# An opening written out engine by engine: attention of three pieces, the first weight halves and TensorE's fillers in one fixed order

## The chip, the cores and the metric

The kernel runs on one core of one Trainium2 chip. The metric is the device time of one execution in microseconds. Before the change it is 868.75 us, the median of three runs (868.51 to 876.98).

## What is computed

Sparse attention over 4 batches, 8 heads, 576 positions and 64 dimensions feeds two feed-forward layers over all 2304 tokens (512 to 2048 to 512), one behind the other. Heads 0 to 3 look at a local window of 32, heads 4 to 7 at positions of the same remainder modulo 32:

```python
scores = np.where(masks, scale * q @ k.T, -1e9); attn = softmax(scores)   # sum + 1e-9
x = (attn @ v).transpose(0, 2, 1, 3).reshape(2304, 512)
h = np.maximum(x @ w_in, 0.0);  x = h * h @ w_out                          # first layer
h = x @ w_in2                                                              # second layer
g = (a0 + a1*h + a2*h**2 + a3*h**3) / (1 + |b0|*|h| + |b1|*h**2 + 1e-6)
out = g @ w_out2
```

The weights arrive as 64-bit floats.

## The kernel before

**Work.** Tokens are cut into six blocks (WIDTHS: 512, 256, then four of 384). For each block j and each of 16 slices f of the hidden width, a unit (j, f) makes 12 products of the first matrix (`h_unit`, line 418: four slices kk of x, each with wh·xh, wh·xl, wl·xh, since every operand is split into a high part that the fast format holds and a low rest), then the square of the ReLU on ScalarE (ACT) and VectorE (DVE), and two units later 12 products of the second matrix (`o_unit1`, line 463). The second layer follows in the same manner (`unit2`). In block 0 a product has 512 columns.

**Attention** goes in 14 pieces, strided ("s") or local ("l"). A piece is scored (`at_scores`: a mask product, line 292, then products of q and k, line 297, into two banks r = 0, 1), normalised bank by bank (`at_softmax`: maximum, subtraction on DVE, exponential on ACT, sum, inverse on DVE, scaling on GpSimd, lines 327 to 341), transposed on TensorE and copied by ACT (`at_transpose`, lines 349, 351), multiplied with v (`at_values`, line 358), and split into xh (a cast on ACT, line 380) and xl (a subtraction on DVE, line 382) by `at_out`. P0, P1 (both strided) and P2 (local) are done ahead of unit (0, 0). P0 and P1 fill the slices kk = 2, 3 of x in block 0, P2 fills kk = 0, 1. The other pieces stand between later units, at the units that the table PLAN names for scores, transposes and values.

**Weights.** `feed_w` takes the halves of the first layer's weights in the order `wq` (first matrix of f, second matrix of f some units behind it): the raw 64-bit words come by DMA, ACT scales the upper word (line 185), DVE joins the bits in three operations (186 to 188), GpSimd makes the high part (197) and the low part (198). Three halves are fed ahead of unit (0, 0), then two per unit.

**What sets the order.** The program is recorded line by line and a scheduling layer then puts the instructions of each engine in order; each engine runs its own queue strictly in that order. Instructions given to `keep_in_program_order` keep the order in which they are written. Before, these are TensorE's instructions of P0 to P2 and the fillers (`fill`, line 486: products of a tile of ones that no one reads, 128x512 in bf16, as many as FILL says at each place). The queue of DMA loads is SP's; a load past `under_way` bytes waits for an earlier one.

Of the kernel before, what the change touches and what calls it, by code (L numbers as in the profile page):

```python
# [9 lines left out]
F32 = mybir.dt.float32  # L10
# [8 lines left out]
P = 128  # L19
# [35 lines left out]
FILL = {'s0': 8, 's1': 1, 't00': 6, 't01': 2, 's2': 2, 't10': 2, 'v1': 4, 't20': 4, 't21': 2, 'h0': 3}  # L55
# [63 lines left out]
def moe_kernel(ctx, tc, qs, vs, ql, vl, w1, w2, a, b, masks, eye, out):  # L119
# [74 lines left out]

    def split_w(wh, wl, wf):
# [78 lines left out]
    def at_scores(p):  # L274

        for r in range(2):
            p.ps[r] = acc_bank(f"ps_s{p.name}_{r}", r == 0 and p.n > HEAD and PLAN[p.n][0][0] == 2)
        late = p.n >= MASK_PE
        fill(f"s{p.n}", p.ps[0])
        masks_ = []  # L280
        for r in range(2):
# [29 lines left out]
        for m in range(p.cb):  # L311
            for hp in range(2):
                for c in range(4):
                    j = 4 * m + c
                    k0 = WIDTHS[p.at] + STARTS[p.at] - _key_start(p.at) + _local_window(p.at, j)
                    for r in range(2):
                        x = p.qk[hp][r * D : (r + 1) * D]
                        score(r, c * STRIDE, 2 * m + hp, x[:, j * STRIDE : (j + 1) * STRIDE], x[:, k0 : k0 + EW])
# [25 lines left out]
    def at_transpose(p, r):  # L344
# [6 lines left out]
        nc.scalar.copy(p.t[r], ps[:, : p.cb * P])  # L351
# [24 lines left out]
    def split_x(parts):  # L376


        for dst, src in parts:
            nc.scalar.copy(dst[0], src)  # L380
        for dst, src in parts:
            nc.vector.tensor_tensor(dst[1], src, dst[0].bitcast(F32), ALU.subtract)

    def at_out(p):
        if not p.strided:
            w = WIDTHS[p.at]
            x_half(0, p.at, 0)
            split_x([(x_rows(0, p.at, hp, w), p.o[hp][:, :w]) for hp in range(2)])
            return
# [16 lines left out]
        split_x([(views, src) for _, views, src in sorted(parts, key=lambda t: t[0])])  # L406
# [75 lines left out]
    def fill(what, ps):  # L482


        for _ in range(FILL.get(what, 0)):
# [5 lines left out]
    load_qk(pieces[1])  # L491
    load_v(pieces[0])
    load(ident, eye)
    load_qk(pieces[2])
# [44 lines left out]
    P0, P1, P2 = pieces[:HEAD]  # L539
    at_scores(P0)  # L540
    at_softmax(P0, 0)
    at_softmax(P0, 1)
    at_scores(P1)
    at_softmax(P1, 0)
    at_transpose(P0, 0)
    at_softmax(P1, 1)
    at_transpose(P0, 1)
    at_scores(P2)
    at_softmax(P2, 0)
    at_values(P0)  # L550
    at_softmax(P2, 1)
    load_qk(pieces[3])
    at_out(P0)
    feed_w(1)
    at_transpose(P1, 0)
    at_transpose(P1, 1)
    at_values(P1)
    at_out(P1)
    load_v(pieces[3])
    feed_w(1)  # L560
    at_transpose(P2, 0)
    at_transpose(P2, 1)
    at_values(P2)
    at_out(P2)
    phase, under_way[0] = 1, 0
    load_raw(fed[0])
    feed_w(1)
# [17 lines left out]
    keep = tc.keep_in_program_order  # L585
# [77 lines left out]
    def unit2(j, f):  # L663
# [105 lines left out]
```

## Time and profile before

| | us |
|---|---|
| median of three runs | 868.75 (868.51 to 876.98) |
| the profiled execution | 869.74 |
| its span, first to last instruction | 868.0 |
| TensorE busy | 857.1 (99%) |
| VectorE, ScalarE, GpSimd busy | 609.8, 482.7, 540.1 |

The profile is of one execution. Times in its rows count from the start of the span, 1.7 us of the execution lie outside it. PE is TensorE's products, PEld its weight loads, DVE is VectorE, ACT ScalarE, POOL GpSimd, SP the engine that issues the DMAs. "Idle before" is the time for which the engine stood still ahead of a row, and what ended it. Rows of several instructions in a row are merged: "0.94 ... x48" is 0.94 us from the first one's start to the last one's end, and products overlap.

### The profile page before, as it was taken

The numbers are of one execution on the slowest core, as the hardware profiler recorded it, in microseconds if no ns is written. First come the engines' busy times: TensorE is split into PE (matmuls) and PEld (weight loads), VectorE is DVE, ScalarE is ACT, GpSimd is POOL, SyncE is SP. The second block draws the span as 40 slices with busy tenths as digits, with TensorE's granted clock in tenths as the row PEclk, the third lists the DMA queues.
The fourth block names the chain that finished last, engine by engine and source line by source line (L and its number), as shares of the span: only waits on it lengthen the run. The fifth ranks groups of instructions, "written<-read, shape, count | busy, mean of one in ns | idle before, by whom it ended". The sixth has DMA issues, their size and how long they took to land.

```text
span 868.0 us, 16453 instructions
## 1 busy us (share of the span) xinstructions
PE 857.1 (99%) x6333; PEld 789.0 (91%) x6338; DVE 609.8 (70%) x791; ACT 482.7 (56%) x1009; POOL 540.1 (62%) x563
## 2 busy tenths in 40 slices
PE   7999999999999999999999999999999999999998
PEld 4788889999999999999999999999999999999996
DVE  6899947635656555452135898888888888888884
ACT  4555633333333334332246877767777767876763
POOL 2677736535554555563324877777777877777773
PEclk9999999999999999999999999999999999999999
DMA  9982345535554445645765200100100100100101
GB/s 330 356 269 90 111 153 186 195 98 172 158 191 154 143 150 189 195 147 184 267 228 208 77 9 10 56 10 10 56 10 10 55 10 10 37 1 0 37 1 37
DMA packets 38959, 100.09 MB, mean 115 GB/s; under 512 B 4576, under 2 KB 10464, under 8 KB 38880
## 3 DMA queue, kind: packets, MB, share of 16 engines
q1 hardware_dynamic: 38880, 99.04, 34.1%
q8 instruction: 50, 0.82, 0.4%
q14 instruction: 29, 0.24, 0.1%
HBM read 72.80 MB, written 26.21 MB: 114 GB/s over the span
## 4 chain that ended last, share of the span: by engine, by line
PE 98%; DVE 1%; POOL 0%; ACT 0%; issue 0%; ACTq 0%; POOLq 0%
PE h L418 46%; PE acc L649 23%; PE acc L463 23%; PE ps_vl L358 1%; PE ps_sl L297 1%; PE ps_vs L358 1%; PE ps_ss L297 1%; PE ps_ts L349 1%; PE ps_tl L349 0%; PE ps_ss L486 0%; DVE sm L327 0%; DVE sm L338 0%; PE ps_tl L486 0%; PE ps_ss L292 0%; DVE eal L336 0%
## 5 line engine op out<-in xcount | busy, mean ns | idle before, releaser
L418 PE MATMUL h<-xh,wh 128*128 128x384 f32 (+2 forms) x768 | 260.4, 339 | 0.7 <-DVE rq L627 0.7
L418 PE MATMUL h<-xh,wl 128*128 128x384 f32 (+2 forms) x768 | 258.1, 336 | 0.0
L418 PE MATMUL h<-xl,wh 128*128 128x384 f32 (+2 forms) x768 | 257.7, 336 | 0.0
L618 DVE RECIPROCAL h<-w 128x384 f32<-128x384 f32 x96 | 245.1, 2553 | 0.7 <-POOL w L615 0.7
L614 POOL TENSOR_TENSOR p<-p,hs 128x384 f32<-128x384 f32 x96 | 98.8, 1029 | 102.4 <-ACT p L612 102.4
L418 PEld LDWEIGHTS h<-xh,wh 128*128 128x128 f32 x768 | 144.8, 189 | 8.2 <-DVE rq L627 1.0
L418 PEld LDWEIGHTS h<-xl,wh 128*128 128x128 f32 x768 | 144.6, 188 | 6.3
L418 PEld LDWEIGHTS h<-xh,wl 128*128 128x128 f32 x768 | 144.4, 188 | 2.6
L463 PE MATMUL acc<-gh,wh 128*128 128x384 f32 (+2 forms) x384 | 128.8, 337 | 0.0
L463 PE MATMUL acc<-gh,wl 128*128 128x384 f32 (+2 forms) x384 | 128.6, 335 | 0.0
L463 PE MATMUL acc<-gl,wh 128*128 128x384 f32 (+2 forms) x384 | 128.6, 335 | 0.0
L441 POOL TENSOR_TENSOR gl<-r,gh 128x384 fp32r<-128x384 f32 (+1 forms) x75 | 74.5, 996 | 73.0 <-ACT gh L440 68.9
L649 PE MATMUL acc<-wh,gl 128*128 128x512 f32 x288 | 113.9, 395 | 0.0
L649 PE MATMUL acc<-wl,gh 128*128 128x512 f32 x288 | 113.7, 395 | 0.0
L649 PE MATMUL acc<-wh,gh 128*128 128x512 f32 x288 | 111.9, 389 | 0.0
L437 DVE TENSOR_TENSOR r<-r 128x384 f32<-128x384 f32 (+1 forms) x75 | 49.5, 661 | 86.6 <-ACT r L433 86.5
L609 ACT ACTIVATE sq<-h 128x384 f32<-128x384 f32 x96 | 47.8, 498 | 105.8 <-PE h L418 101.4
L616 DVE SCALAR_TENSOR_TENSOR p<-p,co,h 128x384 f32<-128x384 f32 x96 | 58.4, 608 | 63.4 <-POOL p L614 63.4
L635 POOL TENSOR_TENSOR gl<-rq,gh 128x384 fp32r<-128x384 f32 x96 | 99.2, 1033 | 2.0 <-ACT gh L634 2.0
L615 POOL TENSOR_TENSOR w<-w,sq 128x384 f32<-128x384 f32 x96 | 98.7, 1029 | 0.0
L433 ACT ACTIVATE r<-h 128x384 f32<-128x384 f32 (+2 forms) x91 | 44.4, 488 | 88.3 <-PE h L418 88.2
L440 ACT CAST gh<-r 128x384 fp32r<-128x384 f32 (+2 forms) x91 | 46.7, 513 | 84.2 <-DVE r L437 83.4
(109 smaller groups left out, 1369.2 us busy)
## 6 DMA issues: line engine op xcount, KB each, us to landing
wraw<-in_w SPq DMA_DIRECT2D x64, 512.0 KB, 4.4
w_scratch<-sph SPq DMA_DIRECT2D x32, 256.0 KB, 3.9
w_scratch<-spl SPq DMA_DIRECT2D x32, 256.0 KB, 3.2
wh<-w_scratch SPq DMA_DIRECT2D x16, 512.0 KB, 3.7
wl<-w_scratch SPq DMA_DIRECT2D x16, 512.0 KB, 4.6
qks<-in_qs SPq DMA_DIRECT2D x8, 585.0 KB, 5.8
xraw<-x_scratch SPq DMA_DIRECT2D x24, 192.0 KB, 2.4
out_dram<-osb SPq DMA_DIRECT2D x18, 256.0 KB, 2.2
```

Of the source, the lines that this page charges most:

```text
L418: nc.tensor.matmul(ps[:, :n], w[:, c], x, start=(kk == 0 and i == 0), stop=(kk == KT - 1 and i == 2))
L437: nc.vector.tensor_tensor(h, h, h, ALU.mult)
L440: last_act = nc.scalar.copy(gh, h).ins
L441: low = lambda: (nc.vector if psum_h or j == 0 else nc.gpsimd).tensor_tensor(gl, h, gh.bitcast(F32), ALU.subtract)
L463: nc.tensor.matmul(acc[j][e][:, : WIDTHS[j]], w[:, c], g, start=(f == 0 and i == 0), stop=(f == NF - 1 and i == 2))
L609: keep(nc.scalar.activation(sq, h, AF.Square))
L614: keep(nc.gpsimd.tensor_tensor(p1, p1, hs, ALU.mult))
L615: keep(nc.gpsimd.tensor_tensor(w, w, sq, ALU.add))
L616: keep(nc.vector.scalar_tensor_tensor(p1, p1, a1, h, ALU.add, ALU.mult))
L618: keep(nc.vector.reciprocal(h, w))
L635: keep(nc.gpsimd.tensor_tensor(gl, rq, gh.bitcast(F32), ALU.subtract))
L649: nc.tensor.matmul(p, g[:, t * P : (t + 1) * P], w[:, c], start=(f == 0 and i == 0), stop=(f == NF - 1 and i == 2))
```

## The change

- The opening is written out: every step of P0, P1, P2 and of the first three weight halves is a call of its own (classes `Soft` and `Half`), and every instruction of it, on each engine, keeps that order.
- TensorE begins with 34 small fillers (64x64 on 32 columns, f32) and five large ones in place of eight large ones; of the other fillers (26 up to the first unit) eight remain.
- P2's first bank is scored ahead of P0's transposes, the second behind them; P2's q and k are loaded ahead of P0's v and of the matrix `ident`. P2's second bank is scaled on DVE, not on GpSimd.
- P2's transposes come ahead of P1's values.
- A weight half of the opening is joined with two DVE operations and one on GpSimd (the sign) in place of three on DVE.
- Unit (0, 0) starts with kk = 2, 3, the strided pieces' slices; the other units of block 0 take kk in the order 2, 3, 0, 1.
- Products for the missing last slot of the strided pieces are left out where a mask product stands ahead (two products each in P0, P1 and the pieces 4 and 5; they wrote what is not used).
- PLAN: the values of piece 6 come at (1, 12) in place of (1, 9), those of piece 9 at (2, 14) in place of (2, 13); with them move the scores of the pieces behind (7 and 10) and piece 9's transposes by one.

```diff
-FILL = {'s0': 8, 's1': 1, 't00': 6, 't01': 2, 's2': 2, 't10': 2, 'v1': 4, 't20': 4, 't21': 2, 'h0': 3}
+KK = (2, 3, 0, 1)
+TINY = {'s0': 34}
+FILL = {'s0': 5, 's1': 1, 's2': 1, 't01': 1, 's2b': 0, 't10': 2, 't20': 2, 'v2': 1}
...
+    class Half:
+        def size(self):
+            self.w = stage.tile([P, DM], I32, tag="w32", bufs=3, name=f"w32_0_{self.f}_{self.part}")
+            keep(nc.scalar.activation(self.w.bitcast(F32), self.hi.bitcast(F32), AF.Abs, scale=2.0**-112))
+        def sign(self):
+            zero = self.hi.bitcast(F32)
+            keep(nc.gpsimd.tensor_scalar(zero, zero, 2.0**-126, 2.0**-126, ALU.mult, ALU.mult))
+        def join(self):
+            bits = psum_w.tile([P, DM], I32, tag="bits", name=f"bits{self.f}_{self.part}")
+            keep(nc.vector.scalar_tensor_tensor(bits, self.w, 3, self.hi, ALU.logical_shift_left, ALU.bitwise_or))
+            keep(nc.vector.scalar_tensor_tensor(self.hi, self.lo, 29, bits, ALU.logical_shift_right, ALU.bitwise_or))
...
+                        if not late and u < 2 * m + s:
+                            continue
...
+        def scale(self, r, engine=None):
+            keep((engine or nc.gpsimd).tensor_tensor(self.ev[r], self.ev[r], self.wide(16 + r * self.n), ALU.mult))
...
+        products = [(kk, i) for kk in (range(KT) if layer else KK) for i in range(3)]
+        if (layer, j, f) == (0, 0, 0):
+            products = [(kk, i) for i, ks in ((0, KK), (1, KK[:2]), (2, KK), (1, KK[2:])) for kk in ks]
...
+        for _ in range(TINY.get(what, 0)):
+            small = warm.bitcast(F32)
+            out = ps[:D, :32]
+            tc.keep_in_program_order(nc.tensor.matmul(out, small[:D, :D], small[:D, :32], start=True, stop=True, skip_group_check=True))
...
     load_qk(pieces[1])
+    load_qk(pieces[2])
     load_v(pieces[0])
     load(ident, eye)
-    load_qk(pieces[2])
...
     at_scores(P1)
-    at_softmax(P1, 0)
+    Soft(P1)
+    P1.soft.most(0)
+    P0.soft.sum(0)
+    P0.soft.inverse(0)
+    P0.soft.scale(0)
+    P1.soft.most(1)
+    P0.soft.sum(1)
...
+    at_scores(P2, (0,))
+    Soft(P2)
     at_transpose(P0, 0)
-    at_softmax(P1, 1)
     at_transpose(P0, 1)
...
+    at_scores(P2, (1,))
+    P2.soft.most(1)
+    P2.soft.less(1)
     at_values(P0)
...
+    P2.soft.scale(1, nc.vector)
+    at_transpose(P2, 0)
+    t_copy(P2, 0)
+    W1 = Half(1)
+    W1.size()
+    W1.sign()
+    at_transpose(P2, 1)
+    t_copy(P2, 1)
     at_values(P1)
...
+    W1.high()
+    early(x_low, P1, slice(None))
     at_values(P2)
+    W1.low()
+    early(x_high, P2, slice(None))
+    early(x_low, P2, slice(None))
+    W2 = Half(2)
...
-        3: ((0, 2), (0, 4), (0, 5)), 4: ((0, 6), (0, 8), (0, 9)), 5: ((0, 10), (0, 12), (0, 13)), 6: ((1, 3), (1, 7), (1, 9)),
+        3: ((0, 2), (0, 4), (0, 5)), 4: ((0, 6), (0, 8), (0, 9)), 5: ((0, 10), (0, 12), (0, 13)), 6: ((1, 3), (1, 7), (1, 12)),
```

On TensorE at the first two units, before (h_0_0 and h_0_1 are the units' banks, xh_0_357 and xl_0_358 come of P0 and P1, xh_0_527 and xl_0_528 of P2; the numbers at a name's end are its place in the program):

```order
L418 MATMUL h_0_0_567<-xh_0_527,wh_0_369 128x512
L418 MATMUL h_0_1_612<-xh_0_527,wh_1_433 128x512
L292 LDWEIGHTS cst
L292 MATMUL ps_sl_0_631<-cst 128x256
L292 LDWEIGHTS cst
L292 MATMUL ps_sl_1_632<-cst 128x256
L418 MATMUL h_0_0_567<-xl_0_528,wh_0_369 128x512
L418 MATMUL h_0_0_567<-xh_0_527,wl_0_370 128x512
L418 MATMUL h_0_0_567<-xh_0_527,wh_0_369 128x512
```
and after, where xh_0_365 and xl_0_366 are of P0 and P1, xh_0_535 and xl_0_536 of P2:

```order
L510 MATMUL h_0_0_577<-xh_0_365,wh_0_445 128x512 x2
L510 MATMUL h_0_1_619<-xh_0_365,wh_1_460 128x512
L510 MATMUL h_0_0_577<-xh_0_535,wh_0_445 128x512
L510 MATMUL h_0_1_619<-xl_0_366,wh_1_460 128x512
L510 MATMUL h_0_0_577<-xh_0_535,wh_0_445 128x512
L510 MATMUL h_0_0_577<-xl_0_366,wh_0_445 128x512 x2
L510 MATMUL h_0_0_577<-xh_0_365,wl_0_446 128x512 x2
L510 MATMUL h_0_0_577<-xh_0_535,wl_0_446 128x512 x2
L510 MATMUL h_0_0_577<-xl_0_536,wh_0_445 128x512 x2
```
The first product of all waits for P2's cast before, and for P0's and P1's after; the scores' masks of piece 3 have moved behind both units.

On VectorE around P2's normalisation, before (ps_sl and eal are P2's two banks, sm the row maxima, sums and inverses, bits and w the first weight half):

```order
L327 TENSOR_REDUCE sm_79<-ps_sl_0_243 128x8
L327 TENSOR_REDUCE sm_80<-ps_sl_1_244 128x8
L336 TENSOR_TENSOR eal_0_314<-ps_sl_0_243,sm_79 128x512
L336 TENSOR_TENSOR eal_1_346<-ps_sl_1_244,sm_80 128x512
L186 TENSOR_SCALAR bits_0_372<-w_0_0_0_371 128x512
L338 TENSOR_REDUCE sm_79<-eal_0_314 128x8
L338 TENSOR_REDUCE sm_80<-eal_1_346 128x8
L339 TENSOR_SCALAR sm_79<-sm_79 128x8
L382 TENSOR_TENSOR xl_0_358<-ps_vs_2_0_321,xh_0_357 128x16x18
L340 RECIPROCAL sm_79<-sm_79 128x8
L339 TENSOR_SCALAR sm_80<-sm_80 128x8
```
and after:

```order
L380 TENSOR_TENSOR eal_0_291<-ps_sl_0_244,sm_81 128x512
L377 TENSOR_REDUCE sm_81<-ps_sl_1_245 128x8
L380 TENSOR_TENSOR eal_1_334<-ps_sl_1_245,sm_81 128x512
L387 TENSOR_REDUCE sm_81<-eal_0_291 128x8
L391 TENSOR_SCALAR sm_81<-sm_81 128x8
L392 RECIPROCAL sm_81<-sm_81 128x8
L387 TENSOR_REDUCE sm_81<-eal_1_334 128x8
L391 TENSOR_SCALAR sm_81<-sm_81 128x8
L392 RECIPROCAL sm_81<-sm_81 128x8
L395 TENSOR_TENSOR eal_1_334<-eal_1_334,sm_81 128x512
L215 SCALAR_TENSOR_TENSOR bits_0_442<-w_0_0_0_390,wraw_0_0_108 128x512
L216 SCALAR_TENSOR_TENSOR wraw_0_0_108<-wraw_0_0_108,bits_0_442 128x512
```
The two banks follow one another instead of going side by side, the second is scaled here (L395), the weights' bits come behind both, and the low parts of P0 and P1 (xl) behind those.

On ScalarE around P2's copies, before (ps_tl to eal: the copies of its transposes; w: the weight halves' scaling):

```order
L185 ACTIVATE w_0_0_1_547<-wraw_0_1_114 128x512
L351 COPY eal_0_314<-ps_tl_0_443 128x512
L351 COPY eal_1_346<-ps_tl_1_453 128x512
L185 ACTIVATE w_0_3_0_559<-wraw_3_0_116 128x512
L380 CAST xh_0_527<-ps_vl_0_461 128x512
L380 CAST xh_0_527<-ps_vl_1_462 128x512
```
and after:

```order
L435 COPY eas_3_0_226<-ps_ts_3_0_378 128x384
L435 COPY eas_3_1_233<-ps_ts_3_1_385 128x384
L207 ACTIVATE w_0_0_0_390<-wraw_0_0_108 128x512
L435 COPY eal_0_291<-ps_tl_0_397 128x512
L207 ACTIVATE w_0_1_0_405<-wraw_1_0_110 128x512
L435 COPY eal_1_334<-ps_tl_1_408 128x512
L462 CAST xh_0_365<-ps_vs_3_0_414 128x16x18
L462 CAST xh_1_367<-ps_vs_3_0_414 128x2x18
L462 CAST xh_0_365<-ps_vs_3_1_415 128x16x15
L462 CAST xh_1_367<-ps_vs_3_1_415 128x2x15
L462 CAST xh_0_535<-ps_vl_0_467 128x512
L462 CAST xh_0_535<-ps_vl_1_468 128x512
```
The scaling of the first two halves has moved to stand ahead of each of P2's copies, and the casts of P1 behind them.

## Rows read from the trace of the kernel before

**Rows 1.** the page, parts 1 and 4: PE, and the chain by engine

```profile
PE 857.1 (99%) x6333; PEld 789.0 (91%) x6338; DVE 609.8 (70%) x791; ACT 482.7 (56%) x1009; POOL 540.1 (62%) x563
...
PE 98%; DVE 1%; POOL 0%; ACT 0%; issue 0%; ACTq 0%; POOLq 0%
```

**Rows 2.** waits of PE from 28 us on: us in total, times, longest

```profile
PE h L418 <- DVE rq L627: 0.7, 1, 0.7
```

**Rows 3.** timeline of PE to 75 us: start, us, line, tiles, shape, count, idle before

```profile
1.49 3.59 PE L486 MATMUL ps_ss<-warm 128*128 128x512 bf16 x8 [1.49 <-DVE warm L481]
4.97 0.72 PE L292 MATMUL ps_ss<-cst 128*128 128x324 bf16 x2
5.62 0.94 PE L297 MATMUL ps_ss<-qks 64*64 64x54 f32 x48
...
7.60 0.92 PE L297 MATMUL ps_ss<-qks 64*64 64x54 f32 x48 [0.43 <-DMA qks<-in_qs]
...
12.26 0.55 PE L349 MATMUL ps_ts<-ident,eas 128*128 128x128 f32 x3 [0.41 <-POOL eas L341]
...
13.60 1.48 PE L297 MATMUL ps_sl<-qkl 64*32 64x64 f32 x128
15.01 0.91 PE L358 MATMUL ps_vs<-eas,vs 54*64 54x54 f32 x44
...
23.54 1.76 PE L358 MATMUL ps_vl<-eal,vl 64*64 64x32 f32 x105 [0.50 <-ACT eal L351]
26.19 0.86 PE L358 MATMUL ps_vl<-eal,vl 64*64 64x32 f32 x21 [0.89 <-issue]
...
27.88 1.42 PE L418 MATMUL h<-xh,wh 128*128 128x512 f32 x2
...
34.70 0.86 PE L297 MATMUL ps_sl<-qkl 64*32 64x64 f32 x64
...
49.72 0.39 PE L463 MATMUL acc<-gh,wh 128*128 128x512 f32 x1
...
52.22 0.39 PE L463 MATMUL acc<-gh,wl 128*128 128x512 f32 x1
```

**Rows 4.** windows: busy us by engine, then PEclk, DMA share, GB/s

```profile
5.00:10.00 5.00, 4.16 (x106) 2.42 (x107) 3.23 (x10) 0.88 (x2) 0.00 (x0) 1.00 1.02 404
...
26.00:27.00 1.00, 0.81 (x22) 0.75 (x23) 0.27 (x1) 0.04 (x1) 0.94 (x1) 0.60 1.05 407
...
29.00:30.00 1.00, 1.00 (x5) 0.81 (x5) 0.96 (x2) 0.00 (x0) 0.45 (x1) 0.70 1.01 344
```

**Rows 5.** timeline of DVE to 45 us

```profile
8.88 0.48 DVE L327 TENSOR_REDUCE sm<-ps_ss 128x6 f32<-128x324 f32 x1
...
16.31 1.28 DVE L336 TENSOR_TENSOR eal<-ps_sl,sm 128x512 f32<-128x512 f32 x2
...
29.50 0.69 DVE L186 TENSOR_SCALAR bits<-w 128x512 int32<-128x512 int32 x1
...
34.27 0.69 DVE L441 TENSOR_TENSOR gl<-r,gh 128x512 fp32r<-128x512 f32 x1 [1.16 <-ACT gh L440]
...
42.33 1.28 DVE L339 TENSOR_SCALAR sm<-sm 128x4 f32<-128x4 f32 x1
```

**Rows 6.** timeline of ACT: the casts of P2

```profile
26.96 1.07 ACT L380 CAST xh<-ps_vl 128x512 fp32r<-128x512 f32 x2 [2.86 <-PE ps_vl L358]
```

**Rows 7.** timeline of POOL (GpSimd)

```profile
25.64 1.30 POOL L198 TENSOR_TENSOR wl<-wraw,wh 128x512 fp32r<-128x512 f32 x1
...
41.95 1.64 POOL L198 TENSOR_TENSOR wl<-wraw,wh 128x512 fp32r<-128x512 f32 x1
...
47.03 1.73 POOL L198 TENSOR_TENSOR wl<-wraw,wh 128x512 fp32r<-128x512 f32 x1
```

**Rows 8.** the DMA queue on SP: the issue of ident

```profile
2.59 0.46 SPq L146 DMA_DIRECT2D ident<-in_eye  x1
```

**Rows 9.** DMA issues to 20 us: KB, median us to landing

```profile
ident<-in_eye SPq DMA_DIRECT2D x1, 64.0 KB, 6.1
```

More of the change, by code (lines that the diff above doesn't have):

```diff
@@ L272, in load_v, with at_scores @@
             p.v.append(t)
-    def at_scores(p):
-        for r in range(2):
+    def at_scores(p, banks=(0, 1)):
+        for r in range(2 if 0 in banks else 0):
             p.ps[r] = acc_bank(f"ps_s{p.name}_{r}", r == 0 and p.n > HEAD and PLAN[p.n][0][0] == 2)
         late = p.n >= MASK_PE
-        fill(f"s{p.n}", p.ps[0])
+        fill(f"s{p.n}" + "b" * (0 not in banks), p.ps[banks[0]])
         masks_ = []
-        for r in range(2):
+        for r in banks:
             flat = p.ps[r][:, : p.nb * p.w]
@@ L310, in at_scores @@
             return
[L311 to L318, printed above, removed]
+        rules = [(m, hp) for m in range(p.cb) for hp in range(2)]
@@ new lines, in at_scores, with __init__, s3, wide @@
+        for m, hp in sorted(rules, key=lambda t: t[1]) if len(banks) == 1 else rules:
+            for c in range(4):
+                j = 4 * m + c
+                k0 = WIDTHS[p.at] + STARTS[p.at] - _key_start(p.at) + _local_window(p.at, j)
+                for r in banks:
+                    x = p.qk[hp][r * D : (r + 1) * D]
+                    score(r, c * STRIDE, 2 * m + hp, x[:, j * STRIDE : (j + 1) * STRIDE], x[:, k0 : k0 + EW])
+    keep = tc.keep_in_program_order
+    class Soft:
+        def __init__(self, p):
+            self.p, self.n, self.sm, self.ev = p, p.nb, sms[p.n], {}
+            p.soft = self
+        def s3(self, r):
+            return self.p.ps[r][:, : self.n * self.p.w].rearrange("p (a k) -> p a k", k=self.p.w)
+        def wide(self, c):
+            return self.sm[:, c : c + self.n, None].to_broadcast([P, self.n, self.p.w])
+        def most(self, r):
+            p, n = self.p, self.n
+            p.e[r] = wpool.tile([P, n, EW], F32, tag="w" + p.homes[r], name=f"ea{p.name}_{r}")
+            if p.strided:
+                keep(nc.gpsimd.memset(p.e[r][:, :, W3:], 0.0))
+            self.ev[r] = p.e[r][:, :, : p.w]
+            keep(nc.vector.tensor_reduce(self.sm[:, r * n : (r + 1) * n], self.s3(r), AX.X, ALU.max))
+        def less(self, r):
+            keep(nc.vector.tensor_tensor(self.ev[r], self.s3(r), self.wide(r * self.n), ALU.subtract))
+        def exp(self, r):
+            keep(nc.scalar.activation(self.ev[r], self.ev[r], AF.Exp, scale=1.0 / 8.0))
+        def sum(self, r):
+            c = 16 + r * self.n
+            keep(nc.vector.tensor_reduce(self.sm[:, c : c + self.n], self.ev[r], AX.X, ALU.add))
+        def inverse(self, *banks):
+            c = self.sm[:, 16 + banks[0] * self.n : 16 + (banks[-1] + 1) * self.n]
+            keep(nc.vector.tensor_scalar(c, c, 1e-9, None, ALU.add))
+            keep(nc.vector.reciprocal(c, c))
+        def scale(self, r, engine=None):
+            keep((engine or nc.gpsimd).tensor_tensor(self.ev[r], self.ev[r], self.wide(16 + r * self.n), ALU.mult))
@@ L350, in at_transpose, with t_copy @@
         p.t[r] = p.e[r].rearrange("p a k -> p (a k)")
-        nc.scalar.copy(p.t[r], ps[:, : p.cb * P])
+        if p.pinned:
+            p.tps = getattr(p, "tps", {})
+            p.tps[r] = ps
+        else:
+            nc.scalar.copy(p.t[r], ps[:, : p.cb * P])
+    def t_copy(p, r):
+        keep(nc.scalar.copy(p.t[r], p.tps[r][:, : p.cb * P]))
     def at_values(p):
@@ L539, in moe_kernel, with early @@
     P0, P1, P2 = pieces[:HEAD]
+    def early(what, p, which):
+        if not hasattr(p, "parts"):
+            p.parts = x_parts(p)
+        what(p.parts[which], keep)
     at_scores(P0)
-    at_softmax(P0, 0)
-    at_softmax(P0, 1)
-    at_scores(P1)
-    at_softmax(P1, 0)
+    Soft(P0)
+    P0.soft.most(0)
+    P0.soft.most(1)
+    P0.soft.less(0)
+    P0.soft.exp(0)
+    P0.soft.less(1)
+    P0.soft.exp(1)
+    at_scores(P1)
+    Soft(P1)
+    P1.soft.most(0)
+    P0.soft.sum(0)
+    P0.soft.inverse(0)
@@ L545, in moe_kernel @@
+    P0.soft.scale(0)
+    P1.soft.most(1)
+    P0.soft.sum(1)
+    P0.soft.inverse(1)
+    P0.soft.scale(1)
+    P1.soft.less(0)
+    P1.soft.exp(0)
+    P1.soft.less(1)
+    P1.soft.exp(1)
+    at_scores(P2, (0,))
+    Soft(P2)
     at_transpose(P0, 0)
-    at_softmax(P1, 1)
     at_transpose(P0, 1)
-    at_scores(P2)
-    at_softmax(P2, 0)
+    t_copy(P0, 0)
+    t_copy(P0, 1)
+    P2.soft.most(0)
+    P1.soft.sum(0)
+    P1.soft.sum(1)
+    P1.soft.inverse(0, 1)
+    P1.soft.scale(0)
+    P1.soft.scale(1)
@@ L550, in moe_kernel @@
+    P2.soft.less(0)
+    P2.soft.exp(0)
+    at_scores(P2, (1,))
+    P2.soft.most(1)
+    P2.soft.less(1)
     at_values(P0)
-    at_softmax(P2, 1)
     load_qk(pieces[3])
-    at_out(P0)
-    feed_w(1)
+    early(x_high, P0, slice(None))
+    P2.soft.exp(1)
+    P2.soft.sum(0)
+    P2.soft.inverse(0)
+    P2.soft.scale(0)
     at_transpose(P1, 0)
+    t_copy(P1, 0)
     at_transpose(P1, 1)
+    t_copy(P1, 1)
+    load_raw(0)
+    W0 = Half(0)
+    W0.size()
+    W0.sign()
+    P2.soft.sum(1)
@@ L557, in moe_kernel @@
+    P2.soft.inverse(1)
+    P2.soft.scale(1, nc.vector)
[6 more added lines that the diff above has]
+    t_copy(P2, 1)
     at_values(P1)
-    at_out(P1)
     load_v(pieces[3])
-    feed_w(1)
-    at_transpose(P2, 0)
-    at_transpose(P2, 1)
-    at_values(P2)
-    at_out(P2)
+    W0.join()
+    W0.high()
+    early(x_low, P0, slice(None))
+    W0.low()
+    early(x_high, P1, slice(None))
+    W1.join()
+    W1.high()
+    early(x_low, P1, slice(None))
@@ L565, in moe_kernel @@
+    at_values(P2)
+    W1.low()
+    early(x_high, P2, slice(None))
+    early(x_low, P2, slice(None))
+    W2 = Half(2)
+    W2.size()
+    W2.sign()
+    W2.join()
+    W2.high()
+    W2.low()
+    fed[0] = 3
     phase, under_way[0] = 1, 0
     load_raw(fed[0])
-    feed_w(1)
     steps = [(j, f) for j in range(NB) for f in range(NF)]
```

38 lines of the change are left out of this document (26 added, 12 removed), and 2 rows, old and new, of the table PLAN.

## The prediction

> **What bounds the kernel now.** I read the page's busy shares and chain first: TensorE (PE) is busy 857.1 us of an 868.0 us span and holds 98% of the chain [rows 1]. The second view is PE's waits from 28 us on: 0.7 us in 840 [rows 2]. So behind 28 us nothing but fewer or faster products can help, and neither is changed there beyond two products left out in each of four strided pieces. What can move is the opening. The third view is PE's timeline [rows 3]: fillers until 4.97, attention of three pieces, the first product of the hidden layer (line 418) at 27.88. The steady pace is 0.227 us a product (49.72 to 52.22 is eleven steps). The first two units, 24 products, and two masks of 256 columns (one more product's worth) are through when line 297 starts at 34.70. At pace they need 25 x 0.227 = 5.7, so the stream "starts" at 29.0, 1.1 later than its first product. The fourth view tells why: the granted clock is 0.60 in 26 to 27 us and back to 1.00 during 29 to 30 [rows 4], so the first products ran at 1.2 GHz.
>
> **The change, part by part, as a walk through the opening.**
>
> *Fillers.* Eight large ones (3.48 us from 1.49 to 4.97, 0.43 each at 1.2 GHz) become 34 small and five large. Before never runs one small tile alone; the nearest rows are the 64x64 value products, four tiles in turn: (1.76-0.22)/105 = 0.0147 each at 2.4 GHz and (0.86-0.29)/21 = 0.027 at 1.2 GHz [rows 3], so 0.059 and 0.109 for a tile. If one tile alone has the round's time, 34 cost 3.7 us; if it has a product's, 0.9. Then five large, 1.1 to 2.1 us. The fillers end between 4.5 and 7.3. I take 3.7, the row that is the same tile, and a clock that rises about where it does now (48 scores from 5.62 take 0.94, 0.015 each after the drain, so the higher level), giving 5.2 + 0.43 + 4 x 0.22 = 6.5: 1.5 later than now.
> The Trainium skill ("TensorE: Matmul & The Clock Gate", section "Wait — 56ns, not 53.3ns?") names a floor of about 62 ns per small matmul when the sequencer decodes it. By that page an estimate for the 34 is 2.1 us and the fillers would end near 5.7; no run here shows it.
>
> *Scores of P0 and P1.* P0's start at 6.8 instead of 5.62. P1's can't start before 7.60 now, where they wait for their DMA [rows 3]; with fillers, masks and P0 ahead they start near 8.1 and end at 9.0. VectorE (DVE) reaches P1's first maximum at 9.25 instead of 8.88, and its written order puts that ahead of P0's sums. So P0's two scalings on GpSimd begin near 10.7 and 12.0 [rows 5].
>
> *Loads.* ident goes behind two 512 KB loads. It was issued at 2.59 and took 6.1, landing at 8.7 [rows 8, 9]; 1.05 MB at 404 GB/s [rows 4] are 2.6 us, so 11.3. P0's first transposes need it, and the scaled scores at 11.45: hidden, with 0.2 to spare. If it lands later, every 1 us costs up to 1 us.
>
> *P2 one bank at a time.* Its first bank is scored before P0's transposes, in PE's wait for GpSimd (10 to 10.9), the second after them. One bank of 64 products costs about 1.0 (128 take 1.48 now). P0's second transposes: 12.75 (now 12.26). Second bank: 13.1 to 14.3. P0's values: 14.4 (now 15.01).
>
> *DVE, ACT, GpSimd behind that.* With 0.6 a step of DVE on 512 columns (16.31, two in 1.28 with the drain of the last) and 0.4 on 324 [rows 5]: P2's maxima 12.6 and 15.2, subtractions 14.6 and 15.8, exponentials 15.3 and 16.7, sums 16.4 and 17.4; the first scaling on GpSimd 17.7 to 18.7, the second now on DVE 18.5 to 19.2. Transposes at 18.8 and 19.3. ScalarE (ACT) has the two weight conversions between P2's copies: copies at 19.4 and 20.7. P1's values run at 19.8 under that. P2's values run from 21.3, where they really begin at 23.54 now, and take 1.9: 23.2. Now they lose 1.0 between the 105 and the 21, with no releaser in the profile; I charge half of that: 23.7. Behind them stood 0.85 of fillers and a wait for P2's cast (26.96 [rows 6]); both go, since the first unit now begins with the strided halves, whose casts and weights (wh from GpSimd at 20.9) are long there. First product: 23.7.
> The trace has a DVE operation of four columns that took 1.28 us at 42.33, while a subtraction on GpSimd ran from 41.95 for 1.64 [rows 5, 7]. The Trainium skill ("SBUF — State Buffer", section "Who interferes with whom") says that a DVE instruction with two SBUF inputs and a GpSimd one that reads SBUF exclude each other for a whole instruction. The scaling moved to DVE is of that kind and meets P2's other scaling and the sign of the weights. By that rule the second transposes could come up to 1.0 later; ACT's conversion ahead of the copy covers 0.3 of it, so the sum would be up to 0.7 worse. The row agrees in kind.
>
> *First products.* kk 0 and 1 wait for P2's casts, two of about 0.6 behind the values, so until 25.0; by then five products (1.1) are done. The stream starts at 24.0.
>
> *Weights.* This is what is late next. The third weight half is now joined behind P2's low part, at 26.4, with two DVE operations in place of three (0.7 less for each of three halves), and the fourth starts at 27.9, 3.9 behind the stream's start. Now that one starts at 29.50 [rows 5], 0.5 behind. So the weights fall 3.4 behind PE. Now their least margin is at the output products of unit 2: wl ends at 47.03 + 1.73 = 48.76 [rows 7] and is used by the third product from 49.72 [rows 3], at 50.17, 1.4 later. DVE gains back 1.2, its idle before 34.27, where it waits for ACT [rows 5]: the first unit ends sooner against it. 3.4 - 1.2 - 1.4 = 0.8 is short; the 1.28 at 42.33 need not come again. I charge 0.6, between 0 and 2.0. Behind it margins are 3 us and more.
>
> *Values one to three units later* (PLAN), the two score products fewer in each of four strided pieces, the order of products in a unit: no wait stands there now [rows 2], they are all PE work that is done anyway: 0. If a place came too early or late, one wait of the size of that 0.7.
>
> **Sum.** 29.0 - 24.0 - 0.6 = 4.4 us less. The profiled execution took 869.74, 868.0 of it the span: 865.3. It lay 1.0 above the median of the three runs, 868.75, so the median after is 864.3. From the ends of the unknown terms: small products at 0.9, no pause in the values, no shortage: 862.6. Fillers to 7.3, the DVE block and the full shortage: 866.9.
>
> **Rivals.**
> - *The clock falls in the sparse middle.* Fillers behind the start drop from 26 to 8. Now it fell once, after a stretch with only the small value products [rows 3, 4]. From 15.6 to 19.8 PE would have 14 transposes and four fillers. If it falls there, P1's and P2's values, 172 at 0.0147, take 0.027 each: 2.1 more. 866.4. For it: the fall that is there now. Against: value products follow at once.
> - *Weights late in earnest.* DVE gains nothing back, the stall is 2.0 in place of 0.6: 865.7. For it: DVE is nearly full there. Against: 1.2 of idle in a row.
> - *Slower: the clock does not rise before the stream.* It decides if the small products keep PE below what lifts the clock and the gaps behind do the same. Then fillers and masks end at 7.8; P0's and P1's scores cost 1.2 each; P2's banks 1.9 each, ending at 17.9 in place of 14.3; transposes and copies double; P2's values start at 25.0 and take 3.5: 28.5. The first 3 us of products at 1.2 GHz lose 1.5: the stream starts at 30.0, 1.0 later than now: 869.8. For it: the first 0.43-us fillers show that the clock starts low. Against: five large fillers and dense scores follow.
> - *It doesn't move the start*: a chain of loads or weights holds the first product near 27.9: 868.7. Against: the second weight half is ready by 26.94 now [rows 7], behind work that moves.
>
> **How the numbers follow.** Forecast 0.53, clock in the middle 0.20, weights 0.13, no effect 0.06, slower 0.08. The first three lie from 862.6 to 867; the range is 862.3 to 867.6, leaving out the last two cases and a little. About 1% (8.7 us) is what a measurement of this kernel can tell from no change. A gain of 8.7 would need the stream at 20.3, before P2's second copy; a loss that large no case gives: within 1% 0.95, faster 0.02, slower 0.03, for a disturbed measurement.
>
> **What would show it.** Right: the first product of the hidden layer between 23 and 24.5 us; small products 0.11 apart; P2's values from about 21.3; a wait of PE for GpSimd's wl below 1 us at the output products of unit 2; no wait behind that but the 0.7. Wrong: a granted clock of half between 15 and 27 us, a first product after 26, or waits for weights in several units.

## The result, and the profile after

| | before | after |
|---|---|---|
| median in one session (18 runs each) | 869.52 (868.46 to 876.98) | 876.24 (872.91 to 878.81) |
| the profiled execution, its span | 869.74, 868.0 | 875.41, 873.6 |

The ratio is 1.0069, 95% interval 1.0053 to 1.0084: slower by 0.7%; the medians lie 6.7 us apart. The forecast was 864.3, and its range ended at 867.6.

The page of after first, its busy share and its chain, for [rows 1]:

```profile
PE 860.9 (99%) x6365; PEld 795.2 (91%) x6369; DVE 607.9 (70%) x787; ACT 482.5 (55%) x1009; POOL 540.7 (62%) x565
PE 89%; DVE 5%; POOL 2%; issue 1%; DMA 1%; ACT 1%; POOLq 0%; DVEq 0%; ACTq 0%
```

PE still holds the chain, with 89% where it held 98%. Where it stood still behind the opening is in PE's waits from 31 us on, for [rows 2]:

```profile
PE h L510 <- DVE rq L786: 1.1, 1, 1.1
PE acc L555 <- POOL gl L533: 0.3, 1, 0.3
PE acc L555 <- POOL wl L232: 0.3, 1, 0.3
PE h L510 <- ACT r L525: 0.2, 1, 0.2
```

Before, 0.7 us stood there; after, 1.9. The rest lies in the opening. PE's timeline of after, for [rows 3]:

```profile
1.48 7.46 PE L580 MATMUL ps_ss<-warm 64*64 64x32 f32 x68 [1.48 <-DVE warm L573]
9.28 1.91 PE L582 MATMUL ps_ss<-warm 128*128 128x512 bf16 x4 [0.33 <-issue]
10.98 0.75 PE L326 MATMUL ps_ss<-cst 128*128 128x324 bf16 x2
11.66 1.53 PE L331 MATMUL ps_ss<-qks 64*64 64x54 f32 x44
...
13.72 0.91 PE L331 MATMUL ps_ss<-qks 64*64 64x54 f32 x44
...
26.88 1.17 PE L442 MATMUL ps_vl<-eal,vl 64*64 64x32 f32 x65
29.68 1.56 PE L442 MATMUL ps_vl<-eal,vl 64*64 64x32 f32 x63 [1.63 <-issue]
31.16 2.07 PE L510 MATMUL h<-xh,wh 128*128 128x512 f32 x4
```

Four things are to be seen. The 34 small products are 68 rows and take 7.46 us (of the five large fillers behind them the trace has four; the first would fill the 0.33 called issue). The masks start at 10.98, 6.0 later than the 4.97 of before. The same 44 rows of scores take 1.53 us at 11.66 and 0.91 at 13.72, so the clock rose between them, at about 13 (the clock's own records begin with a rise at 13.10). And P2's values stand still for 1.63 in their middle, with no releaser. From the masks to the first hidden product the new order takes 20.2 us where the old one took 22.9; it gains 2.7 of the 6.0 back and leaves 3.3.

The granted clock then falls, as in [rows 4], from 30.2 to 33.6 us: about 1 us ahead of the first hidden products and on through them. It is the seventh number of a row, between POOL's count and the DMA share:

```profile
10.00:12.00 2.00, 2.00 (x17) 0.80 (x19) 0.00 (x0) 0.00 (x0) 0.00 (x0) 1.00 1.05 421
...
30.00:32.00 2.00, 2.00 (x57) 1.84 (x50) 0.36 (x3) 0.75 (x2) 1.68 (x2) 0.54 0.91 287
32.00:34.00 2.00, 2.00 (x7) 1.52 (x7) 1.47 (x3) 2.00 (x4) 0.66 (x1) 0.60 1.06 383
34.00:36.00 2.00, 2.00 (x10) 1.66 (x9) 1.83 (x4) 0.22 (x2) 0.73 (x2) 1.00 0.95 295
```

The first of these rows has 1.00 although the scores in it run at the lower pace: ahead of the clock's first recorded change the column shows 1.00, and the mean clock of an execution leaves that stretch out too (0.998 for this one, with 13 us at the lower pace ahead). In the opening the level is therefore read from how long equal rows take.

All kernels of this document have 4,320 hidden and output products, so each can be compared with the product at the same place in the order of before (within the first unit the order differs). How much later (+) or earlier (-) than before it starts in the profiled executions, in us (e2 to e11 are the experiments below):

```
product            0    36    96   264   700  1300  1900  2400  last
start in before 27.9  38.3  53.6  96.9 168.0 279.9 391.5 479.7 863.8
after           +3.3  +3.5  +4.2  +4.6  +4.7  +4.6  +5.2  +5.7  +5.7
e2              +8.8  +8.2  +8.2  +8.2  +9.8  +9.7 +10.3 +10.3 +10.3
e3              +3.4  +2.6  +3.6  +4.1  +6.1  +6.1  +6.4  +6.9  +6.8
e4              -0.6  +0.5  +0.8  +1.7  +3.3  +3.2  +4.7  +5.2  +5.2
e5              -5.4  -1.7  -1.7  -0.9  +0.8  +3.2  +3.2  +3.7  +3.6
e6              -0.5  -0.5  -0.5  +0.4  +2.1  +2.4  +3.0  +3.0  +3.0
e7              +1.9  +1.0  +1.0  +1.4  +2.3  +2.9  +2.9  +2.8  +2.8
e8              -1.5  -2.3  -1.1  -0.6  -0.6  -0.6  -0.6  -0.1  -0.2
e9              -2.0  -1.5  -1.4  -0.6  -0.5  -0.2  -0.2  +0.3  +0.2
e10             -4.7  -4.1  -4.0  -3.1  -3.1  -3.2  -3.1  -2.6  -2.7
e11             -1.9  -2.5  -1.8  -1.3  -1.3  -1.3  -1.1  -0.6  -0.6
```

A row is one execution, and not always a typical one: the traced execution of e7 was the slowest of its twelve (872.6, median 870.2), those of e8 and e11 were the fastest (869.5 and 869.2, medians 871.0 and 871.9), and that of e10 the second fastest (867.1, median 872.8). e1 has no row, because its traced execution was a disturbed one of 2987 us; e5 is the same kernel.

### The profile page after: what moved, and what is told of

It is laid out like the page before. It is cut to its first block, busy times and chain, and to the rows that moved or that the text cites. A ratio compares the mean times of both kernels' runs of the same rounds, so it can differ in the third digit from the quotient of the medians.

```text
span 873.6 us, 16516 instructions
## 1 busy us (share of the span) xinstructions
PE 860.9 (99%) x6365; PEld 795.2 (91%) x6369; DVE 607.9 (70%) x787; ACT 482.5 (55%) x1009; POOL 540.7 (62%) x565
## 4 chain that ended last, share of the span: by engine, by line
PE 89%; DVE 5%; POOL 2%; issue 1%; DMA 1%; ACT 1%; POOLq 0%; DVEq 0%; ACTq 0%
PE h L510 42%; PE acc L808 23%; PE acc L555 19%; DMA w_scratch<-sph 1%; PE ps_vl L442 1%; PE ps_ss L580 1%; PE ps_vs L442 1%; POOL spl L232 1%; PE ps_ss L331 1%; PE ps_sl L331 1%; POOL sph L231 0%; ACT w L187 0%; DVE bits L189 0%; DVE bits L188 0%; DVE wraw L190 0%
```

## The experiments

**e1, e2, e3, e4: one part of the change each.**

```diff
 e1, on after:   -TINY = {'s0': 34}   +TINY = {}            FILL 's0': 5 -> 8
 e2, on before:  +TINY = {'s0': 34}                         FILL 's0': 8 -> 5
 e3, on after:   PLAN as before (piece 6's values at (1, 9), piece 9's at (2, 13))
 e4, on after:   TINY 's0': 34 -> 15                        FILL 's0': 5 -> 0
```

> The changed kernel, with the eight large fillers of before in TensorE's first wait (no small ones), all else kept. Theory A (the small products alone: each runs as two passes of 0.11 us, so 34 take 7.46 us, and the masks of the first scores start at 10.98 instead of 4.97): first scores near 5.6, first product of the hidden layer near 25.5, the whole execution 5 to 6 us faster than the changed kernel, so 868 to 871 us, about the kernel before. Rival B (the written order and the weights behind it hold the time): the start moves, but waits of TensorE for weights take it back, over 873 us. Rival C (PLAN): no change of the waits after 100 us, and the gain is the same as in A less about 1 us.

> The kernel before, with 34 small and five large fillers in place of its eight large ones and nothing else changed. Theory A: fillers end near 11, every step of the opening is late by up to 6.0 us, of which the wait for P1's load (0.43) and a few waits for loads give back 0.5 to 1.5; 873 to 875.5 us, so most of the loss by this one edit. Rival B: the opening has other slack (loads, weights) and the time stays within 2 us of before.

> The changed kernel with the three places of values and scores of PLAN as before. Theory A: no place of the table stands on the path, within 1 us of the changed kernel (875 to 877). Rival C: the later places push work into units that have less room, and 1 to 2 us come back (874 to 875); or they were moved to avoid a wait, and the time grows by 1 us or more.

> The changed kernel with 15 small fillers and no large one: 15 x 0.219 = 3.3 us, so they end at 4.8 us like the eight large ones. Theory A1 (only the length of the fillers costs): the same as the run with eight large ones within 0.7 us. Theory A2 (small products also keep the clock at 1.2 GHz, as the trace of the changed kernel shows it until 13.1 us): the scores and transposes up to the rise take double, and it is 1 to 3 us slower than with eight large ones.

| | median, us | ratio to before, 95% interval |
|---|---|---|
| e1 | 873.36 | 1.0021 (0.9999 to 1.0044) |
| e2 | 879.95 | 1.0089 (1.0060 to 1.0119) |
| e3 | 878.97 | 1.0082 (1.0056 to 1.0109) |
| e4 | 874.05 | 1.0035 (1.0013 to 1.0057) |

With eight large fillers in place of the small ones the change loses less: 1.8 us by the ratio of e1, whose interval reaches 1, and 3.7 by e5 below, the same kernel. Theory A had 868 to 871 for it. Put into before, the small ones cost more than the 873 to 875.5 expected: 8 us by the ratio, 10 by the medians (e2). Without the new table, which I had priced at nothing, the change is slower by another 2.7 by the medians and 1.1 by the ratios, whose intervals overlap (e3 against after); that the table is worth anything is not shown by this. e4 lies 0.7 above e1, on the edge between its two theories, so its trace has to decide. The traces of e2 to e4 say why none of these is a plain sum. e2's opening:

```profile
1.48 7.46 PE L489 MATMUL ps_ss<-warm 64*64 64x32 f32 x68 [1.48 <-DVE warm L482]
...
21.47 0.68 PE L359 MATMUL ps_vs<-eas,vs 54*64 54x54 f32 x30
25.80 0.45 PE L359 MATMUL ps_vs<-eas,vs 54*64 54x54 f32 x14 [3.65 <-issue]
```

The fillers take the same 7.46, and behind them stands a pause of 3.65 us in P0's values, where before had none, with "issue" as its cause: PE waited for nothing that the profile shows. And e4:

```profile
1.48 3.41 PE L580 MATMUL ps_ss<-warm 64*64 64x32 f32 x30 [1.48 <-DVE warm L573]
...
5.75 1.53 PE L331 MATMUL ps_ss<-qks 64*64 64x54 f32 x44
...
8.29 1.53 PE L331 MATMUL ps_ss<-qks 64*64 64x54 f32 x44
...
23.45 3.91 PE L442 MATMUL ps_vl<-eal,vl 64*64 64x32 f32 x128
```

Its small products fill the same time as eight large ones (3.41 for 3.48 us), but both pieces' scores still run at the lower clock, 1.53 us for 44 rows. So the small products did not lift it; it rose at 10.3. It fell again from 20.6 to 30.8, which is why P2's 128 rows of values take 3.91 us here and 2.07 in e5 below. Its line in the table shows something else: from -0.6 at the first product it goes to +5.2. In PE's waits stand a pause of 1.3 in the scores of piece 7 (at 164 us, "issue"), and waits for GpSimd's gl of 1.2 (at 375 us), for ACT's r of 0.6.

**The pauses called issue.** They begin at the same products of the program in every kernel. I count PE's program in passes: a product in bf16 or in the split format is one, an f32 product of scores, values or small fillers two, as it has two rows in the trace. In passes from the program's start:

```
pass 222-223:  e8 0.66  e9 0.50  e10 0.55  e11 0.37
pass 349-351:  e2 3.65  e3 1.48  e7 0.49  e8 1.91  e9 1.74  after 1.02*  e6 1.03*
pass 475-476:  before 0.89  after 1.63  e3 1.67  e8 0.43  e11 1.95  e5 2.44*
pass 1738-39:  in the values and scores of piece 7, a run of 192 short passes;
               passes of the run ahead of it, and the pause (start to start, less 0.11):
               e9 73: 0    e8 77: 0      after 112: 0    e7 143: 0.72  e2 149: 1.45
               e4 155: 1.38  e6 166: 1.54  e5 177: 1.52  e3 184: 1.82  before, e10, e11: behind the run: 0
* put down to an instruction of another engine by the view
```

222, 349 and 476 lie 127 apart. The starred ones at 349 are pauses of this kind at least in part: in after GpSimd's instruction ended at 21.57 and PE went on at 22.27, in e6 ScalarE's ended at 20.09 and PE went on at 20.55. And the page has, under its DMA queues:

```profile
q8 instruction: 50, 0.82, 0.4%
```

50 packets of 16 KB, for 6,369 passes one per 127; from 400 us on they start about 128 products apart. PE went on 2.2 to 2.8 us after the start of such a packet in 24 of 25 pauses (3.2 in e2, where the packet itself took twice as long): 27.38 and 29.68 in after, 23.87 and 26.19 in before. In the openings the packets started 4.3 to 9.6 us apart, mostly 5.5 to 7.5. So I read these pauses as PE without instructions: where many short passes, 15 ns each, run through in 1 to 2 us, the next block isn't there yet. The Trainium skill ("Runtime: NRT & Kernel Launch", section "Instruction fetch mechanics") has the blocks of 16 KiB, 256 instructions, and says that crossing a boundary is mostly hidden; the traces agree on the block (128 products and their 128 weight loads), and on the hiding at most places: of some 50 blocks in an execution, one to four show a pause over 0.3 us. In runs of short passes it was not hidden. This theory was put to the test, as its price is a forecast: whoever adds passes ahead moves all places behind.

**e5, e6, e7: the places moved, and the table alone.**

```diff
 e5: e1 again
 e6, on before:  16 of the 26 large fillers behind the start as 64 products
                 of 128 columns (the same columns, 48 passes more)
 e7, on before:  PLAN of after
```

> The changed kernel with eight large fillers and no small one, once more for its rows. Instruction theory (in the steady part the trace has one 16 KB instruction packet per 128 products with their weight loads, and the pauses called issue fall where such a place comes late in a run of short products; the number of products ahead shifts all these places): the place in the values and scores of piece 7 lies 138 products into a run of 192, so a pause of 1.4 to 1.9 us is there near 155 to 165 us, and none over 0.5 us in the values of P2. Opening theory (the later pauses belong to an engine that is behind): no pause at piece 7, since PLAN is the new one, and one in the values of P2 as in the changed kernel. Both: first product 24.5 to 27.5 us, 871 to 875 us.

> The kernel before, where 16 large fillers (six at t00, two at t10, four at v1, four at t20) are 64 of a quarter of the columns: the same columns, 48 products more, nothing else. Instruction theory: the places of the packets move by 48 products; in the run of piece 7 from 44 and 172 to 124 of 192, so a pause of 1.4 to 1.9 us appears in piece 7's scores near 155 us which the kernel before does not have; first product within 0.7 of 27.9; in all 870.5 to 873. Opening theory: the same columns, so within 0.5 us of before and no pause at piece 7.

> The kernel before with the new table of places alone (three places one to three units later). If the table is worth the 2.7 us that it gave in the changed kernel: 866.5 to 867.5. Instruction theory (the 2.7 were mostly the pause in piece 7 that it moved away): here the place lies at 100 of 192 in piece 7's run instead of 44 and 172, so a pause of up to 1.9 us may come instead and nothing is gained: 869 to 871.5.

e6 is the plainest: 872.69 us, ratio 1.0031 (1.0013 to 1.0048), and the pause is where it was forecast. The run of piece 7 in before, then in e6:

```profile
151.78 1.60 PE L358 MATMUL ps_vl<-el,vl 64*64 64x32 f32 x96
153.31 1.17 PE L297 MATMUL ps_sl<-qkl 64*32 64x64 f32 x96
```

```profile
152.19 1.60 PE L359 MATMUL ps_vl<-el,vl 64*64 64x32 f32 x96
153.72 0.95 PE L298 MATMUL ps_sl<-qkl 64*32 64x64 f32 x70
156.10 0.43 PE L298 MATMUL ps_sl<-qkl 64*32 64x64 f32 x26 [1.44 <-issue]
```

The same products, 0.4 us later and fed by the same engines; what moved is only how many instructions stand ahead of them, 130 us before. The theory that such pauses belong to an engine that is late falls with this run. The pause is about half of what e6 lost; the rest is waits for ACT's r (0.7 at product 264) and GpSimd's gl (0.4), which neither theory had.

e7 gave 870.24 us, 1.0000 (0.9982 to 1.0018), and a pause of 0.6 at piece 7: put into before, the table is worth nothing measurable. In after it moved piece 7 off the place (112 passes ahead in place of 184).

e5 gave 873.38 us, 1.0043 (1.0023 to 1.0063), inside both theories' 871 to 875. Its opening and its waits:

```profile
5.52 0.91 PE L331 MATMUL ps_ss<-qks 64*64 64x54 f32 x44
...
20.51 2.07 PE L442 MATMUL ps_vl<-eal,vl 64*64 64x32 f32 x128
```

```profile
22.51 0.50 PE L510 MATMUL h<-xh,wh 128*128 128x512 f32 x1
25.44 1.37 PE L510 MATMUL h<-xh,wh 128*128 128x512 f32 x3 [2.44 <-ACT w L187]
```

```profile
PE ps_sl L331 <- issue: 1.4, 1, 1.4
PE ps_ss L331 <- issue: 1.3, 1, 1.3
PE h L510 <- DVE rq L786: 1.1, 1, 1.1
PE h L510 <- ACT r L525: 0.6, 1, 0.6
PE acc L555 <- issue: 0.5, 1, 0.5
```

With large fillers the clock is up at 5.5 us, and the first product starts at 22.51, 5.4 earlier than before and 2.0 earlier than forecast. Then PE stands for 2.44. The view puts that down to ACT, but the product stands at pass 475, an instruction packet started at 23.17, and 2.3 us behind it PE went on. About 1.0 of it PE would have waited anyway, as GpSimd's wh for the second unit was ready at 24.0. The clock then fell from 25.6 to 29.0. The pause at piece 7 came as the theory said (1.4); two more that I had not forecast (1.3 at 274 us, 0.5 at 199) and the waits for r and rq took the rest.

**e8 and e9: the change without small products, with passes added to move the places.**

```diff
 e8, on after:  TINY = {}, all 16 large fillers as quarters of 128 columns, 52 more quarters
                ahead of the transposes (100 passes more than e5)
 e9, on after:  TINY = {}, 107 one-pass bf16 products of 32x32 in PE's first waits
                (104 passes more than e5)
```

> The changed kernel without small products: its eight first fillers and its eight others as 64 of a quarter of the columns, and 52 more quarters in front of the transposes, so that 100 products more stand ahead of the stream than with eight large ones. Written-order theory (the order saves what the forecast said, small fillers, a low clock and pauses for instructions took it): clock up from 5 to 6 us to the end, no pause in the values of P2 and none at piece 7, first product 23.5 to 25, in all 865.5 to 868. Rival (weights and activations behind take back any earlier start): first product by 25, but waits for weights and activations of 2 us or more behind it, 868.5 to 871.

> The changed kernel without the 34 small products; instead 107 one-pass bf16 products of 32x32 in TensorE's first waits (48 and five large ones before the masks, 15 before piece 1, 28 before P0's transposes, 16 before P2's), so that 104 products more stand ahead of the stream than with eight large fillers. In all runs so far the pauses came at products 350, 476 and 1738 to 1739 of the program (a product of two passes counted twice), if some 115 or more short ones stood in a row before; here 349 has 86 before it, 476 has 76, and 1739 has some 70. Instruction theory: no issue pause over 0.4 us in the whole span; first product 22.5 to 24, the second within 0.6 of it where it waited 2.4 us with eight large ones. Then, if the pauses were all that took the order's gain: 4 to 5 us ahead of before from the first product to the end, 865 to 866.5. If weights and activations of the first block take an earlier start back: 1 us or less ahead at product 264 and at the end, 868 to 870. If the 2.4 us of the second product was a real wait for ScalarE's sizing of the third weight half: it is there again at 25.4, and 870 to 872.

e8: 871.03 us, 1.0012 (0.9993 to 1.0031). e9: 870.32, 1.0009 (0.9999 to 1.0020). Both are level with before. Piece 7 has no pause in either, as forecast. But the forecast for the opening was wrong for both: the first product came at 26.3 and 25.9, not by 25 and 24, both have pauses, and both medians lie 3 to 4 us above the forecast if the order's gain were kept. e9:

```profile
17.41 0.56 PE L443 MATMUL ps_vs<-eas,vs 54*64 54x54 f32 x21 [1.74 <-issue]
...
27.41 0.73 PE L511 MATMUL h<-xh,wh 128*128 128x512 f32 x2 [0.83 <-POOL wh L225]
```

86 short passes ahead were enough for 1.74 there. With 474 passes ahead of the first hidden product (574 in e8, 578 in e9) and 127 from place to place, three or four places fall into the opening wherever they are moved: the pauses there are 3.0 us in e8 and 2.2 in e9. Whether the packets come 5 to 7 us apart because the supply is no faster, or because PE asks no sooner, isn't shown.

**e10: fewer passes.** 14 of the 22 score products of each of P0 and P1 are left out, with six large fillers in their place. It no longer computes the whole attention and is there for its times alone.

```diff
-                        if not late and u < 2 * m + s:
+                        if not late and (u < 2 * m + s or p.n < 2 and m):
                             continue
```

> The changed kernel with eight large fillers and no small one, where 14 of the 22 score products of each of the first two pieces are left out (28 products, 56 passes; about 1.2 us of TensorE's time) and six large fillers of about the same time stand in their place: 50 passes fewer ahead of the stream, all waits of other engines as they were. Theory of the supply (TensorE pauses where its instructions aren't there yet; passes 350 and 476 of the program): pass 350 comes in the values of P2 with some 100 short ones before it, 476 behind the first 24 hidden products, 1739 behind piece 7; the first product at 22 to 23 us and no pause of 2.4 us behind it, none at piece 7. If the 2.4 us were a wait for ScalarE or GpSimd they are there again at 25.4. What the whole is worth then: if the first block's weights and activations take a lead back whatever its size, 1 us or less is left at product 264, 868 to 869.5; if they don't, 4 to 5 us are left, 864.5 to 866.

The profiled execution took 867.09 us, and its first products are these:

```profile
23.20 0.73 PE L510 MATMUL h<-xh,wh 128*128 128x512 f32 x2
24.76 0.73 PE L510 MATMUL h<-xh,wh 128*128 128x512 f32 x2 [0.84 <-POOL wh L224]
```

The wait of 2.44 is gone, and it was not ACT's: the ACT instruction named in e5 ended at 26.08 here, 1.3 behind PE's start at 24.76. What is left is 0.84 for GpSimd's wh. At product 264 the lead is still 3.1, at the end 2.7: of 4.7 the first block takes 1.5 back, between the two cases of the forecast. Yet the median is 872.76, 1.0027 (1.0009 to 1.0044). Two of the twelve executions had a mean granted clock of 0.999 and took 866.8 and 867.1; the other ten had 0.992 to 0.996 and took 871.2 to 874.1. Before had 0.997 to 1.000 in 16 of its 17. So the clock was down for longer in most executions: 0.003 to 0.007 of 867 us are 2.6 to 6.1 us, which would take the lead and more. That the few large fillers behind the start are the reason is likely and not shown, nor is where in the span the clock fell in those ten, as a trace is of one execution. In e5 the mean clock doesn't sort the executions: the one at 0.998 took 873.4, the seven at 0.992 to 0.996 took 872.6 to 875.9.

**e11: large work in every wait.** After with PLAN of before, no small products, eight large fillers, and 38 fillers of 256 columns, 16 of them ahead of P2's transposes.

> The changed kernel without small products, with the table of places of before: eight large fillers at the start as before, and 38 of half the columns (256) in its other places, most in front of P2's transposes where TensorE waited, so that TensorE runs on through its waits with few instructions. The runs of the kernel with eight large fillers had a mean granted clock of 0.991 to 0.998, of the kernel before 0.998 to 1.000, and of the kernel with fewer passes two runs at 0.999 took 867 and ten at 0.992 to 0.996 took 871 to 874. Clock theory (what is left of the loss is a clock that falls in the opening once its fillers are gone): mean clock 0.998 to 1.000 in most runs. Supply theory: pass 1739 comes behind piece 7, no pause there; pass 476 in the values of P2 with a pause of 0.5 to 2 us. If both hold: first product 23.5 to 25.5, 2 to 3 us ahead of before at product 36, 1 to 2 at the end, 867 to 868.7. If the first block takes all of the lead back: 869 to 870. If filling the waits only moves the end of P2's attention: first product behind 26, 870 to 872.

871.92 us, 1.0014 (0.9996 to 1.0032); the profiled execution 869.22. The clock held better (0.998 or 1.000 in 9 of 12), piece 7 is free, and pass 476 has its pause:

```profile
21.71 1.71 PE L443 MATMUL ps_vl<-eal,vl 64*64 64x32 f32 x100
25.36 0.66 PE L443 MATMUL ps_vl<-eal,vl 64*64 64x32 f32 x28 [1.95 <-issue]
```

It is 2.5 ahead at product 36 and 0.6 at the end. But this is the fastest of the twelve; the eight others at 0.998 took 869.9 to 873.0, so a clock that holds did not bring the forecast 867 to 868.7, and what these lost stays open. No version of this order was measurably faster than before, so there is none to put in its place.

## Why the prediction was wrong

The forecast put the stream of products 5.0 us earlier and lost 0.6 of it: -4.4. The profiled execution of after ends 5.7 later, 10.1 off. Step by step:

- **Fillers: the term that failed.** "If one tile alone has the round's time, 34 cost 3.7 us": they took 7.46. The time of one row was right, 7.46/68 = 0.110 us; but a small product in f32 is two rows, and I had taken rows for products (the 105 and 21 rows of [rows 3] that I divided are with two more 128 rows, which are 64 products). My upper bound for the end of the fillers, 7.3, rested on the same count; they ended at 10.98. The sign I had named, "small products 0.11 apart", came true for the rows and so could not show the error.
- **The clock.** "A clock that rises about where it does now" (5.7 us): about 13. I had this as a rival at 8%, "small products keep PE below what lifts the clock", with the five large fillers and the dense scores as the case against it; e4 and e5 show that the small products were it: with them alone both pieces' 44 rows took 1.53 us, with eight large ones 0.91. (In e11, with eight large ones too, the first piece's still took 1.51.) With the fillers it put P0's scores at 11.66, not 6.8: 4.9 of the 10.1.
- **The order itself was right.** From P0's scores to the first product I had 16.9 us (6.8 to 23.7). e5, with large fillers, has 17.0 (5.52 to 22.51; its wait of 2.44 comes right behind and is not in this figure). In after it is 19.5, with the lower clock at its start and the pause of 1.63, of which I had charged 0.5: 2.6 more.
- **"No releaser in the profile; I charge half of that."** This was the sign of the second cause, and I priced it as chance. It is a place in the program (pass 476). Everything that adds or removes passes ahead moves such places, so the price of an edit like PLAN can't be read from waits alone, as its "0" was.
- **Weights and later waits.** "I charge 0.6, between 0 and 2.0." From product 36 to the end after lost 2.2: 0.7 to product 96 (GpSimd's wl), 0.5 at 264 (ACT's r), 0.6 at about 375 us (gl), 0.5 at 471 us (rq, 1.1 in place of 0.7); the starts move by more than the waits in the view, which add 1.2. Only the first was in the forecast. The 0.5 at rq is in all kernels built on after and in none built on before; why, stays open. The ACT wait at 264 comes in e6 too, which is before with other fillers, so no part of the change is needed for it.
- The rest of the 10.1, about 1, is the clock that the first products were to have and did not (0.54 from 30 us on).
- **Small terms.** The matrix ident, forecast at 11.3 and hidden by 0.2, held P0's transposes in e5 until 11.26 and cost 0.5. The block of DVE by GpSimd came as 0.45: an operation of eight columns at 23.49 took 0.62 in place of 0.17 and ended with GpSimd's scaling at 24.1. The upper end of the sum, 866.9, should be 867.2 by its terms (0.8, 0.7, 1.4); nothing hangs on it.
- **The first rival, "the clock falls in the sparse middle"**, had 0.20 and 2.1 us. In the traced execution of after it didn't happen; the clock fell at 30.2. It did between 12 and 31 us in those of e3, e4, e7 and e9. Of the 18 executions of after the two with a mean clock of 1.000 took 872.9 and 873.2, the sixteen at 0.993 to 0.998 took 873.9 to 878.8. So some 3 of the 6.7 us may be a clock that falls for longer, and the rest stands without it; where it fell in those sixteen isn't shown.

In the traced execution the change thus paid 6.0 for its fillers, got 2.7 back by its order, and lost 2.4 behind. Without its small products it is level with before (e8, e9, e11) or 3.7 us slower (e5), by where its passes fall and, as far as the runs show, by how the clock holds.

## What to carry to other kernels

Count products in the program's own order and rows in the trace, and divide one by the other, before a row's time is used as a product's. A run of about a hundred or more short passes can be held up by the supply of instructions (86 to 184 ahead of a place cost 0.7 to 1.8 us here, 112 at another nothing): find the places from one trace (here every 127 or 128 passes), and ask of each edit ahead of such a run how many passes it shifts them, since a filler at 1 us can cost 1.5 us at 155. Fillers that are to bring the clock up should be few long products, not many short ones: only the long ones did it here, and they cost the fewest instructions as well.

## What the runs showed of the hardware that was not expected

- A TensorE pause of 0.4 to 3.7 us at fixed passes of the program (222, 349, 476, 1738), ending 2.2 to 2.8 us behind the start of a 16 KB instruction packet (3.2 in e2); the views name it "issue", and in e5 a ScalarE instruction that ended at about the same moment.
- 68 rows of 64x32 in f32, back to back for 7.46 us, or 30 for 3.41, did not bring TensorE to the higher clock; with eight rows of 128x512 in bf16, 3.6 us long, it was there at 5.1 to 7.0 us (before, e5, e6, e7, e11). Whether the size or the type makes the difference isn't shown.
- With the same program, executions at a mean granted clock of 0.999 and of 0.992 to 0.996 differed by 4 to 7 us of 867 (e10), somewhat more than the 2.6 to 6.1 that the mean clock makes of it. In e5 no such order is to be seen.
